# tanh(softplus(h)) by sigmoid, arctan and sine, four blocks at a time, in a fused attention and expert kernel

## The chip, the cores and the metric

The kernel runs on one core of a Trainium2 chip. A core has TensorE (PE: matrix products, results in PSUM), ScalarE (ACT: functions from a loaded table), VectorE (DVE), GpSimd (POOL) and SyncE (SP, which issues DMAs). Each engine takes its own instructions in the order in which they were written into its queue and waits where one of them is not ready. PSUM has 8 banks of 512 fp32 words per partition. The metric is the device time of the whole program in microseconds (us).

## The reference, cut to what matters

Three parts follow each other: an attention in which a query sees only the keys of its own cluster, a layer of 8 experts in which each token takes the one that its gate chooses, and a dense layer:

```
def _moe2_ref(x, w_in, w_out):
    h = x @ w_in                      # 1536 x 512 by 512 x 2048
    sp = np.where(h > 20.0, h, np.log1p(np.exp(np.minimum(h, 20.0))))
    g = h * np.tanh(sp)
    return g @ w_out                  # 1536 x 2048 by 2048 x 512
```

The change is in the line `g = h * np.tanh(sp)` alone. tanh(log(1 + e^h)) equals ((1 + e^h)^2 - 1) / ((1 + e^h)^2 + 1).

## The kernel before, in words

Every fp32 operand of a product is kept as two fp16 parts, a high and a low one, and a product is three matmuls (high by high, high by low, low by high), so that most results leave PSUM twice: ACT writes the high part, then DVE or POOL subtracts it and writes the low part.

The dense layer handles the 1536 tokens in six column groups q of 256 tokens (`QW`), three for each of the two batches. For one q, `h_units` makes 16 blocks of 128 x 256 (`f`, the rows of h); a block is 12 matmuls with the weights `win` (tile `h`, line 1005 in `mm3`). Two blocks fill one PSUM bank, and four such banks are in turn (`ps_2` has bufs=4). For every block a generator `mish` is put on the list `pend`, and `advance` moves all of them on by one step as the next blocks are written down. Its steps are: exp of h on ACT (L1097, tile `u`), a clamp on POOL (L1098), then on ACT the square (1 + e^h)^2 (L1103, tile `m`), Ln (L1105) and Exp of its negative (L1106, tile `L`: the reciprocal); on DVE h times a term (L1104, tile `hn`, the last reader of the PSUM bank), and one correction step of the reciprocal (L1109, L1110); on POOL the product (L1111); last the high part on ACT (L1115) and the low part on POOL (L115, in `psub`). The result goes to `gsl`, which lies in the tiles `xb` and `gx`. `o_units` multiplies it with `wout` (L1160, tile `o`, 24 matmuls for every four blocks) and writes the rows out (L1165, L1167).

The dense layer of the first column groups runs beside the expert layer of the second batch (`moe1`): its products are the tile `eps` (also L1005; two PSUM banks in turn), and their results leave through ACT (L963, L982) and DVE (L967, L989). The weights of an expert come by DMA in 512 KB pieces (`wf`) and are split by ACT (L916) and DVE (L920). In the same time `convs` turns `w_out` from 64-bit numbers into fp16 parts, in 16 pieces (L1025 to L1028 and L1033 on DVE, L1031 on ACT), and `gate(1)` sorts the tokens of the second batch (L700, L711, L718). The order in which all this is written down is set by `mix`, which takes the next unit from the part that is furthest behind its share. From there a scheduler orders the instructions of each engine, all but SP's, by its own timeline. So where a DVE instruction waits, or takes long, everything written behind it on DVE waits too.

All functions in the kernel before are in one table of ACT, loaded once (L560, at the start). `rest` repeats the computation for tokens over a capacity; its loops run no trip in the profiled execution.

Of the kernel before, what the change touches and what calls it, by code (L numbers as in the profile page):

```python
# [19 lines left out]
P = 128  # L20
# [4 lines left out]
def clustered_attention_moe_kernel(  # L25
# [110 lines left out]
    nc.gpsimd.memset(cst[:, 0:1], 1.0)  # L136
    nc.gpsimd.memset(cst[:, 1:2], -2.0794415416798357)
    mcol = cp.tile([P, OV], F32, name="mcol")
# [931 lines left out]
    def open_second():  # L1070
        m_p["m1"] = ctx.enter_context(tc.tile_pool(name="m1", bufs=1, side="right"))
        m_p["m2"] = ctx.enter_context(tc.tile_pool(name="m2", bufs=2, side="right"))
        m_p["ps"] = ctx.enter_context(tc.tile_pool(name="ps_2", bufs=4, space=PSUM, side="right"))
        m_p["wout"] = m_p["m1"].tile([P, 2, NF, DM], F16, name="wout")
        gx = m_p["m1"].tile([P, 8, 2, QW], F16, name="gx")
        nx = (T * ROW) // (2 * QW)
        for b in range(2):
            v_ = xb[b].rearrange("p t r -> p (t r)")[:, 0:nx * 2 * QW].rearrange("p (n a w) -> p n a w", a=2, w=QW)
            gsl[b] = [v_[:, n] for n in range(nx)] + [gx[:, 4 * b + n] for n in range(NF - nx)]

    pend = []
    g_done = set()
    C20 = 485165195.40979

# [6 lines left out]

    def mish(pt, gg, key, w_=QW):

        m2 = m_p["m2"]
        yield
        u = m2.tile([P, QW], F32, tag="u", name="u", bufs=3)[:, 0:w_]
        nc.scalar.activation(out=u, in_=pt, func=AF.Exp, scale=2.0 ** -17)  # L1097
        nc.gpsimd.tensor_scalar(out=u, in0=u, scalar1=C20, scalar2=0.0, op0=ALU.min, op1=ALU.max)  # L1098
        yield
        m = m2.tile([P, QW], F32, tag="n", name="m", bufs=4)[:, 0:w_]  # L1100
        L = m2.tile([P, QW], F32, tag="L", name="L", bufs=3)[:, 0:w_]
        hn = m2.tile([P, QW], F32, tag="hn", name="hn", bufs=4)[:, 0:w_]
# [10 lines left out]
        if key:  # L1113
            assert key[0] < 2 or (key[0] - 2, key[1] // 4) in o_done, key
        nc.scalar.activation(out=gg[:, 0], in_=hn, func=AF.Copy)  # L1115
        psub(gg[:, 1], hn, gg[:, 0])
        g_done.add(key)

# [4 lines left out]
    def h_units(q):  # L1123
# [4 lines left out]
        for f in range(NF):  # L1128
            while q > 1 and (q - 2, f // 4) not in o_done:
                yield None  # L1130
            if f % 2 == 0:
                h_t[q] = m_p["ps"].tile([P, 2, QW], F32, tag="h", name="h")
            pt = h_t[q][:, f % 2]
            mm3(pt, win, x1[:, :, :, p * QW:(p + 1) * QW], CD, slice(f * P, (f + 1) * P))
# [12 lines left out]
    def o_units(q):  # L1147
# [3 lines left out]
        for f4 in range(NF // 4):  # L1151
# [5 lines left out]
            for t in range(NQ):  # L1157
                for f in range(4 * f4, 4 * f4 + 4):
                    for i_, (a, c) in enumerate(((0, 0), (0, 1), (1, 0))):
                        nc.tensor.matmul(pts[t], lhsT=gsl[q % 2][f][:, a, t * P:(t + 1) * P], rhs=wout[:, c, f, :], start=(f == 0 and i_ == 0), stop=(f == NF - 1 and i_ == 2))  # L1160
                if t == NQ - 1:
                    o_done.add((q, f4))
                if f4 == NF // 4 - 1:
                    ob = m_p["m2"].tile([P, DM], F32, tag="ob", name="ob")
                    nc.scalar.activation(out=ob, in_=pts[t], func=AF.Copy, scale=-2.0 ** -17)  # L1165
                    tt = p * NQ + t
# [7 lines left out]
    def rest():  # L1174
# [194 lines left out]
```

## Time and profile before

| what | value |
|---|---|
| time, median of 3 runs | 718.24 us (718.12 to 718.4) |
| time of the profiled execution | 716.69 us |
| its span, first to last instruction | 715.0 us |
| mean granted TensorE clock | 0.962 |
| PE busy | 618.3 us (86%) |
| DVE busy | 545.8 us (76%) |
| ACT busy | 469.8 us (66%) |
| POOL busy | 448.7 us (63%) |

The shares are averages over parts of the program that have different limits: the attention takes about the first 340 us, the experts of the first batch lie partly in it, and the dense layer runs from 342.5 us to 706.3 us. PE's busy time counts every matmul that is on its way, so the cost of a matmul is read from the time between starts in a row of equal ones, not from the mean of one.

### The profile page before, as it was taken

The numbers are of one execution on the slowest core, as the hardware profiler recorded it, in microseconds if no ns is written. First come the engines' busy times: TensorE is split into PE (matmuls) and PEld (weight loads), VectorE is DVE, ScalarE is ACT, GpSimd is POOL, SyncE is SP. The second block draws the span as 40 slices with busy tenths as digits, with TensorE's granted clock in tenths as the row PEclk, the third lists the DMA queues.
The fourth block names the chain that finished last, engine by engine and source line by source line (L and its number), as shares of the span: only waits on it lengthen the run. The fifth ranks groups of instructions, "written<-read, shape, count | busy, mean of one in ns | idle before, by whom it ended". The sixth has DMA issues, their size and how long they took to land.

```text
span 715.0 us, 15063 instructions
## 1 busy us (share of the span) xinstructions
PE 618.3 (86%) x5618; PEld 409.0 (57%) x5619; DVE 545.8 (76%) x1047; ACT 469.8 (66%) x980; POOL 448.7 (63%) x516
## 2 busy tenths in 40 slices
PE   1697989976678895988998978799999999999995
PEld 1365767744356553654765555556666666776542
DVE  6889887899999999789969999996543356465400
ACT  2577888876467775664658786768755678777500
POOL 5578797995955656551276757656565577777711
PEclk9899999999689998999999999989999999999999
DMA  7542352413833332345344443351100000000000
GB/s 227 134 92 64 91 162 60 109 45 97 280 83 93 95 108 75 119 148 160 108 165 161 148 143 93 95 174 58 45 16 0 1 30 1 31 1 16 17 30 33
DMA packets 56753, 64.52 MB, mean 90 GB/s; under 512 B 10080, under 2 KB 46944, under 8 KB 56672
## 3 DMA queue, kind: packets, MB, share of 16 engines
q1 hardware_dynamic: 42064, 48.74, 24.1%
q10 hardware_dynamic: 12688, 8.42, 3.9%
q0 software_dynamic: 1920, 6.32, 2.3%
q8 instruction: 47, 0.77, 0.5%
q14 instruction: 34, 0.28, 0.1%
HBM read 46.23 MB, written 6.32 MB: 73 GB/s over the span
## 4 chain that ended last, share of the span: by engine, by line
PE 44%; DVE 34%; issue 9%; DMA 5%; ACT 4%; POOL 3%; SPq 1%; POOLq 0%; DVEq 0%; ACTq 0%
PE h L1005 13%; PE o L1160 11%; PE eps L1005 8%; DVE mxh L349 4%; DVE w L920 3%; DVE f L1026 3%; DMA wf<-in_moe_w_dram 2%; DVE f L1028 2%; PE s L389 2%; DVE mxh L354 2%; DVE f L1025 2%; DVE win L1033 2%; DVE oT L299 2%; PE x L348 1%; DVE m L363 1%
## 5 line engine op out<-in xcount | busy, mean ns | idle before, releaser
L115 POOL TENSOR_TENSOR el<-e,eh 128x768 f16<-128x768 f32 x86 | 146.7, 1716 | 62.5 <-ACT eh L398 36.2
L1005 PE MATMUL h<-x,win 128*128 128x256 f16 x1152 | 132.3, 273 | 0.0
L1005 PEld LDWEIGHTS <-win 128*128 128x128 f16 x1152 | 112.6, 98 | 19.1
L1005 PEld LDWEIGHTS <-w 128*128 128x128 f16 x768 | 75.5, 99 | 76.2 <-issue 22.8
L1111 POOL TENSOR_TENSOR hn<-hn,L 128x256 f32<-128x256 f32 x96 | 79.1, 826 | 34.9 <-DVE L L1110 33.3
L1160 PE MATMUL o<-wout,xb 128*128 128x512 f16 x432 | 96.7, 381 | 0.0
L391 ACT ACTIVATE e<-s 128x384 f32<-128x384 f32 x152 | 70.3, 486 | 27.4 <-PE s L389 23.4
L1005 PE MATMUL eps<-xw,w 128*128 128x416 f16 x384 | 76.9, 351 | 12.8 <-DVE x L989 6.2
L389 PE MATMUL s<-QK 128*128 128x384 f16 x320 | 81.5, 345 | 4.2 <-ACT e L391 4.0
L398 ACT ACTIVATE eh<-e 128x768 f16<-128x768 f32 x88 | 73.9, 845 | 16.9 <-PE av L427 7.9
L1109 DVE SCALAR_TENSOR_TENSOR m<-m,L 128x256 f32<-128x256 f32 x96 | 54.1, 565 | 38.0 <-ACT L L1106 37.1
L1098 POOL TENSOR_SCALAR u<-u 128x256 f32<-128x256 f32 x96 | 49.8, 519 | 52.5 <-ACT u L1097 46.5
L1005 PE MATMUL eps<-hT,w 128*128 128x416 f16 x384 | 72.5, 342 | 2.7 <-DVE hT L967 1.7
L115 POOL TENSOR_TENSOR xb<-hn,xb 128x256 f16<-128x256 f32 x72 | 57.4, 800 | 21.9 <-ACT xb L1115 20.1
L1160 PEld LDWEIGHTS <-xb 128*128 128x128 f16 x432 | 42.5, 98 | 48.8 <-issue 1.2
L425 PE MATMUL av<-vst,eh 128*128 128x65 f16 x528 | 64.0, 198 | 6.2 <-DVE xt L440 4.9
L349 DVE TENSOR_REDUCE mxh<-x 128x1 f32<-128x512 f32 x96 | 63.5, 674 | 4.9 <-PE x L348 4.7
L427 PE MATMUL av<-vst,el 128*128 128x65 f16 x528 | 61.3, 197 | 5.2 <-POOL el L115 4.6
L426 PE MATMUL av<-vst,eh 128*128 128x64 f16 x528 | 64.0, 199 | 0.0
L1104 DVE SCALAR_TENSOR_TENSOR hn<-m,h 128x256 f32<-128x256 f32 x96 | 39.3, 412 | 31.5 <-ACT m L1103 30.5
L1103 ACT ACTIVATE m<-u,cst 128x256 f32<-128x256 f32 x96 | 48.1, 502 | 20.2 <-POOL u L1098 19.0
L425 PEld LDWEIGHTS <-eh 128*128 128x128 f16 x528 | 51.1, 100 | 15.2 <-DVE xt L440 7.4
(227 smaller groups left out, 1316.4 us busy)
## 6 DMA issues: line engine op xcount, KB each, us to landing
wf<-in_moe_w_dram ACTq DMA_DIRECT2D x16, 512.0 KB, 4.5
raw<-in_moe_w_in_dram SPq DMA_DIRECT2D x16, 512.0 KB, 3.8
raw<-in_moe_w_out_dram SPq DMA_DIRECT2D x16, 512.0 KB, 3.6
wf<-in_moe_w_dram SPq DMA_DIRECT2D x16, 512.0 KB, 4.4
QK<-hl SPq DMA_DIRECT2D x32, 192.0 KB, 3.1
xs<-dr SPq DMA_DIRECT2D x12, 258.0 KB, 3.0
t<-in_k_dram SPq DMA_DIRECT2D x8, 384.0 KB, 4.1
t<-in_q_dram SPq DMA_DIRECT2D x8, 384.0 KB, 3.4
```

Of the source, the lines that this page charges most:

```text
L115: nc.gpsimd.tensor_tensor(out=out_, in0=in0, in1=in1, op=ALU.subtract)
L349: nc.vector.reduce_max(out=mx_t[i][:, t, 0:1], in_=sp, axis=AX.X)
L389: nc.tensor.matmul(sps[hf][:, 0:HS], lhsT=st[:, KA + a, kt * P:(kt + 1) * P], rhs=st[:, QA + a, hf * HS:(hf + 1) * HS], start=(a == 0), st ...
L391: nc.scalar.activation(out=e32[:, hf * HS:(hf + 1) * HS], in_=sps[hf][:, 0:HS], func=AF.Exp, scale=1.0 / float(D) ** 0.5)
L398: nc.scalar.activation(out=eh, in_=e32, func=AF.Copy)
L425: nc.tensor.matmul(av[:, t, :], lhsT=eh[:, cols], rhs=vs[:, h, 0:NV], start=(kt == 0 and t == 0), stop=False, skip_group_check=True)
L426: nc.tensor.matmul(av[:, t, 0:D], lhsT=eh[:, cols], rhs=vs[:, h, NV:], start=False, stop=False, skip_group_check=True)
L427: nc.tensor.matmul(av[:, t, :], lhsT=el[:, cols], rhs=vs[:, h, 0:NV], start=False, stop=(kt == T - 1), skip_group_check=True)
L1005: nc.tensor.matmul(out_, lhsT=wc[:, a, kk, ms], rhs=mv[:, c, kk, :], start=(i == 0), stop=(i == n - 1))
L1109: nc.vector.scalar_tensor_tensor(out=m, in0=m, scalar=1.0, in1=L, op0=ALU.add, op1=ALU.mult)
L1111: nc.gpsimd.tensor_tensor(out=hn, in0=hn, in1=L, op=ALU.mult)
L1160: nc.tensor.matmul(pts[t], lhsT=gsl[q % 2][f][:, a, t * P:(t + 1) * P], rhs=wout[:, c, f, :], start=(f == 0 and i_ == 0), stop=(f == NF - ...
```

## The change

tanh(log(1 + e^h)) is now computed as sin(2 arctan(sigmoid(h - log 2))). With s = e^h / (2 + e^h) the sine of twice the arctangent is 2s / (1 + s^2), which is the same fraction as before. ACT does sigmoid, arctan and sine, DVE one product with h, ACT and POOL the high and low part. The clamp and the correction step are gone. The work is grouped: one `mish` for four blocks, whose `h` tile takes two PSUM banks (two such tiles in turn, the same four banks in all). The sigmoid runs in two halves of 128 x 512, one for each bank; arctan, sine, the product and both parts are single instructions of 128 x 1024. Sigmoid and arctan are in one table of ACT and the sine in another, so that a group loads a table twice.

```
-    def mish(pt, gg, key, w_=QW):
+    def mish(pt, gg, q, k, n=FB, w_=QW):
         m2 = m_p["m2"]
-        yield
-        u = m2.tile([P, QW], F32, tag="u", name="u", bufs=3)[:, 0:w_]
-        nc.scalar.activation(out=u, in_=pt, func=AF.Exp, scale=2.0 ** -17)
-        nc.gpsimd.tensor_scalar(out=u, in0=u, scalar1=C20, scalar2=0.0, op0=ALU.min, op1=ALU.max)
-        yield
...
-        nc.scalar.activation(out=m, in_=u, func=AF.Square, bias=cst[:, 0:1])
-        nc.vector.scalar_tensor_tensor(out=hn, in0=m, scalar=-1.0, in1=pt, op0=ALU.add, op1=ALU.mult)
-        nc.scalar.activation(out=L, in_=m, func=AF.Ln, bias=cst[:, 0:1])
-        nc.scalar.activation(out=L, in_=L, func=AF.Exp, scale=-1.0, bias=cst[:, 1:2])
-        yield
-
-        nc.vector.scalar_tensor_tensor(out=m, in0=m, scalar=1.0, in1=L, op0=ALU.add, op1=ALU.mult)
-        nc.vector.scalar_tensor_tensor(out=L, in0=m, scalar=-0.25, in1=L, op0=ALU.add, op1=ALU.mult)
-        nc.gpsimd.tensor_tensor(out=hn, in0=hn, in1=L, op=ALU.mult)
-        yield
...
-        nc.scalar.activation(out=gg[:, 0], in_=hn, func=AF.Copy)
-        psub(gg[:, 1], hn, gg[:, 0])
+        s = m2.tile([P, FB, QW], F32, tag="s", name="s", bufs=3)[:, 0:n, 0:w_]
+        hf = max(n // 2, 1)
+        for u in range(0, n, hf):
+            nc.scalar.activation(out=s[:, u:u + hf], in_=pt[:, u:u + hf], func=AF.Sigmoid, scale=2.0 ** -17, bias=cst[:, 1:2])
+            if u + hf < n:
+                yield
+                yield
+        nc.scalar.activation(out=s, in_=s, func=AF.Arctan)
+        nc.scalar.activation(out=s, in_=s, func=AF.Sin, scale=2.0)
+        yield
+        nc.vector.scalar_tensor_tensor(out=s, in0=s, scalar=2.0 ** -6, in1=pt, op0=ALU.mult, op1=ALU.mult)
+        yield
...
+        nc.scalar.activation(out=gg[:, :, 0], in_=s, func=AF.Copy)
+        psub(gg[:, :, 1], s, gg[:, :, 0])
...
-            if f % 2 == 0:
-                h_t[q] = m_p["ps"].tile([P, 2, QW], F32, tag="h", name="h")
...
-            pend.append(mish(pt, gsl[q % 2][f], (q, f)))
-            next(pend[-1])
+            if f % FB == 0:
+                h_t[q] = m_p["ps"].tile([P, FB, QW], F32, tag="h", name="h", bufs=2)
...
+            if f % FB == 1:
+                pend.append(mish(h_t[q], gsl[q % 2][f // FB], q, f // FB))
+                next(pend[-1])
```

In the changed kernel the lines are L1101 (sigmoid), L1105 (arctan), L1106 (sine), L1108 (product on DVE) and L1111 (high part).

On ACT, at the first column group of the dense layer, this stands in the kernel before (`u`, `m` and `L` are the steps of the blocks of tile `h_5713` and of the next one, `wout` is a piece of `w_out`):

```order
L1097 ACTIVATE u_5738<-h_5713 128x256
L910 ISA
L910 DMA wf_6182<-in_moe_w2_dram 128x8x128
L1103 ACTIVATE m_5837<-u_5738,cst_112 128x256
L1105 ACTIVATE L_5838<-m_5837,cst_112 128x256
L1106 ACTIVATE L_5838<-L_5838,cst_112 128x256
L1097 ACTIVATE u_5844<-h_5713 128x256
L1097 ACTIVATE u_5869<-h_5824 128x256
```

and at the same place after the change (`s_5738` belongs to the first group of four, in `h_5713`, and `s_5935` to the second, in `h_5907`):

```order
L1101 ACT_TABLE_LOAD
L1101 ACTIVATE s_5738<-h_5713,cst_112 128x512
L910 ISA
L910 DMA wf_6082<-in_moe_w2_dram 128x8x128
L1101 ACTIVATE s_5935<-h_5907,cst_112 128x512
L1031 ACTIVATE wout_5627<-f32_6076 128x512
L1101 ACTIVATE s_5738<-h_5713,cst_112 128x512
L1105 ACTIVATE s_5738<-s_5738 128x1024
L1106 ACT_TABLE_LOAD
L1106 ACTIVATE s_5738<-s_5738 128x1024
L1101 ACT_TABLE_LOAD
L1101 ACTIVATE s_5935<-h_5907,cst_112 128x512
```

The first half of the second group's sigmoid now stands ahead of the second half of the first group's, so that the first group's banks are held until PE has done half of the second group. Two table loads stand in every group, 48 for the 24 groups.

On DVE, a little later, where the expert layer's last two `hT` pieces of the first batch are written, this stands in the kernel before:

```order
L967 SCALAR_TENSOR_TENSOR hT_5683<-eps_6090,hT_5683 128x416
L1176 CAST nf_10174<-nblk_139 128x16
L1109 SCALAR_TENSOR_TENSOR m_5974<-m_5974,L_5975 128x256
L1177 TENSOR_REDUCE nf_10174<-nf_10174 128x1
L1104 SCALAR_TENSOR_TENSOR hn_6047<-m_6045,h_5929 128x256
L1110 SCALAR_TENSOR_TENSOR L_5975<-m_5974,L_5975 128x256
L1178 TENSOR_SCALAR nblk_139<-nf_10174 128x1
L967 SCALAR_TENSOR_TENSOR hT_5683<-eps_6108,hT_5683 128x416
L920 SCALAR_TENSOR_TENSOR w_6381<-wf_6088,w_6381 128x1024
```

and after the change:

```order
L1108 SCALAR_TENSOR_TENSOR s_5738<-s_5738,h_5713 128x1024
L967 SCALAR_TENSOR_TENSOR hT_5683<-eps_6015,hT_5683 128x416
L1108 SCALAR_TENSOR_TENSOR s_5935<-s_5935,h_5907 128x1024
L967 SCALAR_TENSOR_TENSOR hT_5683<-eps_6033,hT_5683 128x416
L920 SCALAR_TENSOR_TENSOR w_6253<-wf_6013,w_6253 128x1024
```

Each of the two `hT` pieces now stands behind one group's product, which itself is behind that group's sine on ACT.

## Rows read from the trace of the kernel before

**Rows 1.** Busy time by stage; the columns are named in the first line.
```profile
core 0: us, PE busy (x) PEld busy (x) DVE busy (x) ACT busy (x) POOL busy (x), PEclk, DMA share, GB/s
342.50:394.10 51.60, 47.35 (x398) 34.91 (x397) 44.00 (x129) 35.57 (x85) 31.07 (x42) 1.00 0.42 138
394.10:463.90 69.80, 58.45 (x396) 38.53 (x395) 67.93 (x115) 51.59 (x116) 48.23 (x56) 0.99 0.39 121
463.90:545.00 81.10, 81.05 (x509) 50.52 (x509) 53.02 (x97) 56.57 (x133) 46.30 (x66) 0.97 0.21 66
545.00:664.70 119.70, 119.70 (x826) 80.64 (x824) 65.33 (x130) 87.08 (x220) 85.84 (x134) 1.00 0.04 14
664.70:706.30 41.60, 41.60 (x194) 18.69 (x192) 6.27 (x12) 9.59 (x23) 12.81 (x18) 1.00 0.04 15
```

**Rows 2.** PE's waits from 342.5 to 463.96 us: total us, times, longest.
```profile
PE eps L1005 <- DVE hT L967: 5.9, 4, 3.2
PE o L711 <- DVE dg L700: 4.2, 5, 1.5
PE eps L1005 <- DVE x L989: 3.7, 1, 3.7
PE eps L1005 <- ACT L L1105: 1.8, 2, 0.9
```

**Rows 3.** Timeline of PE around 460 us: start, length, instruction, idle before.
```profile
455.86 4.38 PE L1005 MATMUL eps<-hT,w 128*128 128x416 f16 x24
463.95 4.32 PE L1005 MATMUL eps<-xw,w 128*128 128x416 f16 x12 [3.71 <-DVE x L989]
```

**Rows 4.** Timeline of PE from 649 to 664.8 us.
```profile
649.06 5.40 PE L1005 MATMUL h<-x,win 128*128 128x256 f16 x48
654.30 5.34 PE L1160 MATMUL o<-wout,gx 128*128 128x512 f16 x24
```

**Rows 5.** ACT's groups, 342.5 to 463.9 us: count, busy us, mean ns, idle before.
```profile
L1103 ACT ACTIVATE m<-u,cst 128x256 f32<-128x256 f32 x30 | 15.0, 503 | 4.0 <-POOL u L1098 3.2 <-DVE goh L738 0.6
L1106 ACT ACTIVATE L<-L,cst 128x256 f32<-128x256 f32 x29 | 14.5, 502 | 0.2
L1105 ACT ACTIVATE L<-m,cst 128x256 f32<-128x256 f32 x29 | 14.4, 501 | 0.3
L916 ACT ACTIVATE w<-wf 128x1024 f16<-128x1024 f32 x12 | 12.7, 1055 | 1.8 <-DMA wf<-in_moe_w_dram 1.8
L1097 ACT ACTIVATE u<-h 128x256 f32<-128x256 f32 x30 | 10.4, 379 | 7.0 <-DVE hn L1104 6.9
L1115 ACT ACTIVATE xb<-hn 128x256 f16<-128x256 f32 x24 | 9.8, 410 | 8.2 <-POOL hn L1111 8.0
```

**Rows 6.** DVE's groups in the same stretch.
```profile
L1109 DVE SCALAR_TENSOR_TENSOR m<-m,L 128x256 f32<-128x256 f32 x29 | 17.7, 616 | 1.5 <-ACT L L1106 1.5
L920 DVE SCALAR_TENSOR_TENSOR w<-wf,w 128x1024 f16<-128x1024 f32 x12 | 17.5, 1460 | 0.3 <-ACT w L916 0.3
L1110 DVE SCALAR_TENSOR_TENSOR L<-m,L 128x256 f32<-128x256 f32 x29 | 13.7, 476 | 0.2
L1104 DVE SCALAR_TENSOR_TENSOR hn<-m,h 128x256 f32<-128x256 f32 x29 | 11.7, 407 | 0.3 <-ACT m L1103 0.3
```

**Rows 7.** POOL's groups: two of the same stretch, one of the attention.
```profile
L1111 POOL TENSOR_TENSOR hn<-hn,L 128x256 f32<-128x256 f32 x29 | 27.2, 942 | 15.0 <-DVE L L1110 14.2 <-DVE gm L766 0.4
L115 POOL TENSOR_TENSOR xb<-hn,xb 128x256 f16<-128x256 f32 x24 | 22.2, 934 | 10.2 <-ACT xb L1115 9.9
...
L115 POOL TENSOR_TENSOR el<-e,eh 128x768 f16<-128x768 f32 x86 | 146.7, 1716 | 62.5 <-ACT eh L398 36.2 <-PE s L389 10.1 <-issue 6.7
```

**Rows 8.** The one table load: duration ns (least, median, most), start.
```profile
L560 ACT ACT_TABLE_LOAD  x1: 1283/1283/1283, 0.8 to 0.8; - x1
```

**Rows 9.** ACT's copy of 128x512 from PSUM, 545 to 664.7 us.
```profile
L1165 ACT ACTIVATE ob<-o 128x512 f32<-128x512 f32 x6 | 3.5, 592 | 2.6 <-PE o L1160 2.6
```

**Rows 10.** Timeline of ACT: two instructions that follow each other without a wait.
```profile
646.00 0.49 ACT L1103 ACTIVATE m<-u,cst 128x256 f32<-128x256 f32 x1
646.40 0.49 ACT L1106 ACTIVATE L<-L,cst 128x256 f32<-128x256 f32 x1
```

More of the change, by code (lines that the diff above doesn't have):

```diff
@@ L136, in clustered_attention_moe_kernel @@
     nc.gpsimd.memset(cst[:, 0:1], 1.0)
-    nc.gpsimd.memset(cst[:, 1:2], -2.0794415416798357)
+    nc.gpsimd.memset(cst[:, 1:2], -0.6931471805599453)
     mcol = cp.tile([P, OV], F32, name="mcol")
@@ L1078, in open_second @@
             v_ = xb[b].rearrange("p t r -> p (t r)")[:, 0:nx * 2 * QW].rearrange("p (n a w) -> p n a w", a=2, w=QW)
-            gsl[b] = [v_[:, n] for n in range(nx)] + [gx[:, 4 * b + n] for n in range(NF - nx)]
+            assert nx % FB == 0 and NF - nx <= FB
+            gsl[b] = [v_[:, n:n + FB] for n in range(0, nx, FB)] + [gx[:, FB * b:FB * (b + 1)]]
     pend = []
     g_done = set()
-    C20 = 485165195.40979
+    FB = 4
     def advance():
@@ L1159, in o_units @@
                     for i_, (a, c) in enumerate(((0, 0), (0, 1), (1, 0))):
-                        nc.tensor.matmul(pts[t], lhsT=gsl[q % 2][f][:, a, t * P:(t + 1) * P], rhs=wout[:, c, f, :], start=(f == 0 and i_ == 0), stop=(f == NF - 1 and i_ == 2))
+                        nc.tensor.matmul(pts[t], lhsT=gsl[q % 2][f // FB][:, f % FB, a, t * P:(t + 1) * P], rhs=wout[:, c, f, :], start=(f == 0 and i_ == 0), stop=(f == NF - 1 and i_ == 2))
                 if t == NQ - 1:
@@ L1164, in o_units @@
                     ob = m_p["m2"].tile([P, DM], F32, tag="ob", name="ob")
-                    nc.scalar.activation(out=ob, in_=pts[t], func=AF.Copy, scale=-2.0 ** -17)
+                    nc.scalar.activation(out=ob, in_=pts[t], func=AF.Copy, scale=2.0 ** -17)
                     tt = p * NQ + t
@@ L1223, in rest @@
                 for f in range(NF):
-                    pt = ps2.tile([P, P], F32, tag="h", name="h")
-                    mm3(pt, win, x1, CD, slice(f * P, (f + 1) * P))
-                    for _ in mish(pt, gsl[0][f][:, :, 0:P], None, P):
+                    pt = ps2.tile([P, 1, P], F32, tag="h", name="h", bufs=2)
+                    mm3(pt[:, 0], win, x1, CD, slice(f * P, (f + 1) * P))
+                    for _ in mish(pt, gsl[0][f // FB][:, f % FB:f % FB + 1, :, 0:P], None, f, 1, P):
                         pass
@@ L1230, in rest @@
                     for i_, (a, c) in enumerate(((0, 0), (0, 1), (1, 0))):
-                        nc.tensor.matmul(po, lhsT=gsl[0][f][:, a, 0:P], rhs=wout[:, c, f, :], start=(f == 0 and i_ == 0), stop=(f == NF - 1 and i_ == 2))
+                        nc.tensor.matmul(po, lhsT=gsl[0][f // FB][:, f % FB, a, 0:P], rhs=wout[:, c, f, :], start=(f == 0 and i_ == 0), stop=(f == NF - 1 and i_ == 2))
                 ob = m2.tile([P, DM], F32, tag="ob", name="ob")
-                nc.scalar.activation(out=ob, in_=po, func=AF.Copy, scale=-2.0 ** -17)
+                nc.scalar.activation(out=ob, in_=po, func=AF.Copy, scale=2.0 ** -17)
                 nc.gpsimd.indirect_dma_start(out=out, out_offset=bass.IndirectOffsetOnAxis(ap=iu[:, 1:2], axis=0), in_=ob, in_offset=None, bounds_check=NT - 1, oob_is_err=False)
```

12 lines of the change are left out of this document (4 added, 8 removed).

## The prediction

> **What bounds the kernel now.** I read the busy times by stage first, because the shares over the whole span say nothing here: nothing before 342.5 us belongs to the changed code, and there the order of PE is the same in both kernels. From 463.9 us to 706.3 us PE is busy without a gap (81.05 of 81.1, 119.7 of 119.7, 41.6 of 41.6 us) [rows 1]. What another engine saves there is worth nothing, and only a new wait of PE would show. In the two stages from 342.5 to 463.9 us PE is busy 47.35 + 58.45 = 105.8 of 121.4 us, and in the second of them DVE is busy 67.93 of 69.8 us [rows 1]. So 15.6 us is what PE loses in all.
>
> Second, who releases PE there: hT on DVE 5.9 us, dg on DVE 4.2, x on DVE 3.7, ACT's Ln 1.8, together 15.6 us [rows 2]. All but the last name DVE. PE waits for a short DVE instruction that stands in a full queue. Third, the timeline after the longest of these waits: 12 matmuls of the form eps took 4.32 us there, where 24 had taken 4.38 us just before [rows 3]. That is the lower of the clock's two levels (1.2 against 2.4 GHz) after PE had stood still for 3.71 us; the granted clock of that stage is 0.97 where the neighbours have 0.99 and 1.00 [rows 1]. It costs 4.32 - 2.19 = 2.1 us. So at most 15.6 + 2.1 = 17.7 us can be had. A kernel without any wait of PE behind 342.5 us would end at about 716.7 - 17.7 = 699 us.
>
> **The change, part by part.** DVE: a block now costs L1109, L1110 and L1104, 616 + 476 + 407 ns, in that stretch 17.7 + 13.7 + 11.7 = 43.1 us [rows 6]. The two column groups that lie there make eight groups of four, and each gets one product of 128x1024. Its nearest row is L920, the same operation at that width, 1.46 us [rows 6]; four of the L1104, which read PSUM as it does, make 1.63 us. With 1.5 us the eight cost 12 us. DVE loses 43 - 12 = 31 us of the 112 us that it is busy in the two stages [rows 1] and is no longer the bound.
>
> POOL: a block now has the product (942 ns), the low part (934 ns) and the clamp. What is left is one low part for four blocks, between 1.72 us (the 128x768 form) and 4 x 0.93 = 3.7 us [rows 7]. POOL waits less, and nobody waits for it: only what o needs much later comes from there.
>
> ACT: a block now costs 379 + 503 + 501 + 502 + 410 ns, so four blocks 9.18 us [rows 5]. A group after the change has two sigmoids of 128x512, arctan, sine and the copy at 128x1024, and two table loads. No row shows the three functions. For the sigmoid the nearest row is the copy of 128x512 from PSUM, 0.59 us [rows 9], plus what an operand for the bias adds (L1103 with one takes 503 ns and L1097 without one 379 ns [rows 5], 0.12 us): 0.71 us. At 128x1024 the nearest row is L916, 1.055 us [rows 5]. So the group takes 1.42 + 3.17 us. The load has one row, 1.283 us [rows 8], and I take that, 2.57 us for two. The sum is 7.15 us, 2.0 us below before. Instructions that follow each other without a wait start 0.40 us apart where each lasts 0.49 [rows 10], so both sums are a little high. The Trainium skill, "ScalarE: Activation LUTs", section "Step-by-step: what each stage is for", says that each function takes the same time per element; no run here shows it yet.
>
> The lower end for the functions is the plain copy, and an upper end would be four times the 128x256 rows, 4 x 0.50 = 2.0 us at 128x1024. A group would then cost 2 x 1.0 + 2 x 2.0 + 1.64 + 2.57 = 10.2 us, 1.0 us more than before. I take the wide row, since L916 shows directly what that width costs.
>
> From 545 us on, PE needs 10.4 us for a group (48 matmuls of h start 5.24 us before 24 of o, which take 5.2 [rows 4]). ACT's 7.15 us, and 0.3 us for the copies of o, lie beneath that. In that part a group's banks are wanted again only after 24 o, 48 h and 24 o, 15.6 us after its last matmul. The way from that matmul to the end of the product is 0.71 + 1.06 + 1.28 + 1.06 + 1.5 = 5.6 us. It fits, and so nothing is won or lost behind 463.9 us.
>
> In the stage from 342.5 to 463.9 us ACT has 35.57 + 51.59 = 87.2 us of work [rows 1], of which 15.0 + 14.5 + 14.4 + 10.4 + 9.8 = 64 us (and 1.7 us of the same copies into gx) is this function's [rows 5]. After: 8 x 7.15 = 57 us, so about 79 us beside 106 us of matmuls.
>
> What is late next, then? I followed the order after the change with these durations through the first groups. The first group's second sigmoid stands behind the first one of the second group. That one waits 4.4 us from the first group's last matmul (7 eps, the 12 small ones of the ranks and 24 h lie between), and then come 0.71, a wout piece (0.6, as [rows 9]), 0.71, 1.06, 1.28, 1.06 and the product's 1.5: 11.3 us. PE asks for the banks after 48 h, 24 eps and the ranks, 5.2 + 4.4 + 0.5 = 10.1 us. That is a wait of 1 us, or 3 where DVE is not free. The last hT piece of the first batch stands on DVE behind the product of the second group, and PE's last three matmuls that use it come about 1 us early. In the part where the second batch's first expert runs, ACT's half of hT stands up to 0.71 + 1.06 + 1.28 + 1.06 = 4.1 us behind a group's sigmoid, arctan, load and sine, but between two eps of the same bank stand 12 other eps (2.2 us) and 12 to 27 h (1.3 to 3 us), so that a wait of under 1 us is left, a few times. The waits for the sorted rows' DMA behind dg stay (about 1 us), and so may one for expert weights. I put 7 us of waits in place of the 17.7 us and get a gain of 10.5 us.
>
> The profiled execution took 716.69 us (span 715.0 and 1.7 around it), which is 1.55 us under the median of 718.24. So 716.7 - 10.5 = 706.2 us on the profile's scale, and **707.7 us** as the median of runs. The likeliest case's own range is 703 to 713, from 15 down to 5 us of gain.
>
> **The rivals.**
> First, that a table load costs more than its row. The one load stood at the program's start with nothing before it on ACT; in the new places it stands between instructions that overlap now (0.49 us long, 0.40 apart [rows 10]), and what the engine does not start while the load waits for the one before it is in no row. If each load holds ACT for twice its row, the 16 loads of the stage add 16 x 1.28 = 20.5 us: 99 us of work on an engine that also waits for PE and DVE. It idles 121.4 - 87.2 = 34 us there now; if half of that remains, the stage lasts 99 + 17 + 2.6 (until the first half group is there) = 118.6 us, 2.8 us less than now, and the time is 715.4 us, between 712 and 719. Behind 545 us the group would take 9.7 us of 10.4 and still fit. For it: the loads are in order and cannot overlap. Against it: the row itself is a complete load.
> The Trainium skill, "ScalarE: Activation LUTs", section "What ACT_TABLE_LOAD costs", gives 1283 ns for the load, as the trace has it, and another 1380 ns for a drain ahead of it, 2.66 us for each switch; by that an estimate for 16 loads is 22 us more on ACT, and the time would be this rival's. No run here shows the drain.
>
> Second, slower: the banks are held too long. With two tiles of two banks PE can be one group ahead; before, it could be three tiles ahead and each was free after one exp, a clamp, a square and one DVE product. A group's way to the end of its product is 5.6 us at best, and 48 h matmuls fill only 5.2 us of it. Whatever stands before it on ACT (the last group's copy 1.06, a split of weights 1.06, a load 1.28, an hT 0.5: 3.9 us) is waited for by PE unless eps or dg lie between. It decides from 17.7 / 8 = 2.2 us of wait per group on. With 2.7 us in each of eight groups, and the low clock's 2.1 us after one of them, it costs 21.6 + 2.1 = 23.7 us against 17.7: 6 us slower, 724 us, from 720 to 727. For it: the first group, as followed above. Against it: in these stages 24 eps or 24 dg matmuls stand between the two halves of most groups, which is 2 to 4 us of cover each.
>
> Third, no change: DVE's waits come back as ACT's. hT, x and xw all pass through ACT before DVE, and ACT's instructions in front of them become twice to four times as long. If PE's 15.6 us stay as they are under ACT's name, the time is 718 us, 716.8 to 719.5. For it: PE's one wait for ACT now is for an Ln of this function (1.8 us [rows 2]). Against it: ACT has less to do than DVE had, 79 us against 112.
>
> **How the numbers follow.** Forecast 0.60, expensive loads 0.17, held banks 0.15, no change 0.08. Faster or slower begins at 0.2% (1.4 us), which is what a measurement of this kernel can tell from none. The forecast is faster in all its range; of the expensive loads 0.11 lies under 716.8 us, 0.04 within and 0.02 above; of no change 0.06 within and 0.01 on each side; held banks is slower. Faster 0.71 (0.60 + 0.11, rounded down for the last), same 0.10, slower 0.19. The low end, 701, leaves 1.7 us of waits over the floor on the runs' scale (699 + 1.55); the high end, 720, takes in the expensive loads and no change, and leaves out most of held banks.
>
> **What would show it.** Right: DVE's busy time falls by about a quarter of 112 us between 342 and 460 us; PE's waits for hT and x on DVE shrink to about 1 us each; the dense stage that is now free of gaps starts about 10 us earlier and still has none; the sigmoid lasts about 0.7 us, arctan and sine about 1.05, a load 1.28 with under 0.3 us of other idle time beside it. Wrong: a gap of 1 us or more on ACT around each load (first rival); waits of h on the product L1108 of more than 2 us, again and again (second); waits of eps on ACT's L963 or L982 that add up to 15 us (third); or any gap of PE behind the expert layer.

## The result, and the profile after

The changed kernel takes **708.07 us** (median of 4 runs, 704.72 to 709.14) against 718.18 us for the kernel before beside it (4 runs, 717.21 to 718.4). The ratio is 0.9843, with a 95% interval from 0.981 to 0.9877: 10.1 us faster, where 10.5 us had been forecast. A control later gave 707.39 us.

The profiled execution took 704.72 us. Its attention ended 2 us earlier than before's, which is no part of the change (its order of PE is the same). So I compare the *dense stage*: from the start of the first product of h to the end of the last product of o. It took 363.7 us before (342.5 to 706.2) and 354.2 us after (340.5 to 694.7), 9.5 us less; the control had 354.2 us again.

Busy times by stage after, which answer to [rows 1] and have its columns:

```profile
340.50:390.50 50.00, 47.19 (x399) 34.78 (x397) 37.08 (x107) 38.06 (x52) 14.62 (x12) 1.00 0.46 152
390.50:454.80 64.30, 58.06 (x395) 38.31 (x394) 54.01 (x70) 47.56 (x62) 10.30 (x5) 1.00 0.48 156
454.80:545.00 90.20, 90.20 (x581) 56.73 (x580) 22.15 (x27) 52.90 (x63) 16.89 (x11) 1.00 0.12 36
545.00:652.00 107.00, 107.00 (x740) 72.12 (x738) 11.56 (x11) 70.37 (x75) 25.46 (x16) 1.00 0.04 16
652.00:694.40 42.40, 42.40 (x210) 20.43 (x209) 2.44 (x2) 10.27 (x12) 7.20 (x5) 1.00 0.04 13
```

In the first two stages PE is busy 105.25 us (105.8 before), but of 114.3 us instead of 121.4: it idles 9.05 us where it idled 15.6. DVE falls from 111.9 to 91.1 us, ACT from 87.2 to 85.6, POOL from 79.3 to 24.9. From 454.8 us on PE has no gap. The granted clock is 1.00 in all five; the low clock after the long wait [rows 3] is gone. Over the dense stage PE's idle time fell by 6.6 us (15.65 to 9.05) and its busy time by 2.9 us (348.05 to 345.15).

PE's waits from 342 us to the end, against [rows 2] (total us, times, longest):

```profile
PE eps L1005 <- DVE hT L967: 3.6, 4, 2.1
PE h L1005 <- ACT s L1101: 2.8, 4, 1.2
PE h L1005 <- DVE s L1108: 1.5, 2, 0.8
PE o L711 <- DVE dg L700: 1.1, 1, 1.1
```

The wait for x (3.7 us) is gone, hT and dg are smaller, and h now waits, 4.3 us in all: 1.5 us for the last reader of its banks (L1108), and 2.8 us for a sigmoid (L1101). ACT's groups of the function over the dense stage, against [rows 5] and [rows 8]:

```profile
L1101 ACT ACTIVATE s<-h,cst 128x512 f32<-128x512 f32 x48 | 33.0, 687 | 62.6 <-PE h L1005 62.4
L1101 ACT ACT_TABLE_LOAD x24 | 30.8, 1283 | 2.4 <-PE h L1005 2.0
L1106 ACT ACT_TABLE_LOAD x24 | 30.8, 1283 | 0.4
L1106 ACT ACTIVATE s<-s 128x1024 f32<-128x1024 f32 x24 | 25.4, 1057 | 0.3
L1105 ACT ACTIVATE s<-s 128x1024 f32<-128x1024 f32 x24 | 25.3, 1056 | 0.7
```

DVE's and POOL's groups from 340.5 to 454.8 us, against [rows 6] and [rows 7]:

```profile
L1026 DVE SCALAR_TENSOR_TENSOR f<-raw,f 128x512 int32<-128x512 int32 x16 | 17.9, 1122 | 0.3
L920 DVE SCALAR_TENSOR_TENSOR w<-wf,w 128x1024 f16<-128x1024 f32 x13 | 16.5, 1272 | 0.2 <-ACT w L916 0.2
...
L1108 DVE SCALAR_TENSOR_TENSOR s<-s,h 128x1024 f32<-128x1024 f32 x7 | 8.6, 1222 | 12.2 <-ACT s L1106 12.2
...
L115 POOL TENSOR_TENSOR xb<-s,xb 128x1024 f16<-128x1024 f32 x6 | 13.5, 2247 | 43.6 <-ACT xb L1111 43.5
```

L1026 splits the weights of wout and has nothing to do with the change. Its mean is 1122 ns, and the reason is in the next timelines (start, length, instruction, idle before): first POOL's only instruction from 410 to 425 us, then DVE, ACT and PE beside it.

```profile
418.00 2.12 POOL L115 TENSOR_TENSOR xb<-s,xb 128x1024 f16<-128x1024 f32 x1 [19.09 <-ACT xb L1111]
```
```profile
418.16 2.51 DVE L1026 SCALAR_TENSOR_TENSOR f<-raw,f 128x512 int32<-128x512 int32 x1
420.70 0.69 DVE L1028 SCALAR_TENSOR_TENSOR f<-raw,f 128x512 int32<-128x512 int32 x1
422.09 0.69 DVE L1033 SCALAR_TENSOR_TENSOR wout<-f,wout 128x512 f16<-128x512 f32 x1 [0.69 <-ACT wout L1031]
422.70 0.58 DVE L967 SCALAR_TENSOR_TENSOR hT<-eps,hT 128x416 f16<-128x416 f32 x1
```
```profile
421.43 0.63 ACT L1031 ACTIVATE wout<-f 128x512 f16<-128x512 f32 x1 [3.51 <-DVE f L1028]
421.97 0.50 ACT L963 ACTIVATE hT<-eps 128x416 f16<-128x416 f32 x1
```
```profile
423.34 2.27 PE L1005 MATMUL eps<-xw,w 128*128 128x416 f16 x12 [2.13 <-DVE hT L967]
```

L1026 starts 0.16 us after POOL's subtraction and ends 0.55 us after it (420.12 to 420.67): it lasts 2.51 us instead of 0.69, as if it stood still until POOL had ended. L1028 follows it, ACT's wout piece waits 3.51 us for that, ACT's hT stands behind the wout piece, and PE loses 2.13 us, its longest wait.

### The profile page after: what moved, and what is told of

It is laid out like the page before. It is cut to its first block, busy times and chain, and to the rows that moved or that the text cites. A ratio compares the mean times of both kernels' runs of the same rounds, so it can differ in the third digit from the quotient of the medians.

```text
span 703.1 us, 14009 instructions
## 1 busy us (share of the span) xinstructions
PE 616.4 (88%) x5618; PEld 408.3 (58%) x5619; DVE 433.1 (62%) x783; ACT 448.4 (64%) x668; POOL 299.1 (43%) x252
## 4 chain that ended last, share of the span: by engine, by line
PE 42%; DVE 32%; issue 9%; ACT 6%; DMA 5%; POOL 2%; SPq 1%; POOLq 0%; DVEq 0%; ACTq 0%
PE h L1005 12%; PE o L1157 12%; PE eps L1005 7%; DVE mxh L349 4%; DVE f L1026 4%; DVE w L920 3%; DVE f L1028 2%; DMA QK<-oT 2%; PE s L389 2%; DVE oT L299 2%; DVE mxh L354 2%; DVE f L1025 2%; DVE win L1033 2%; PE x L348 1%; DMA wf<-in_moe_w_dram 1%
## 5 line engine op out<-in xcount | busy, mean ns | idle before, releaser
L1108 DVE SCALAR_TENSOR_TENSOR s<-s,h 128x1024 f32<-128x1024 f32 x24 | 29.3, 1221 | 167.7 <-ACT s L1106 165.1
L115 POOL TENSOR_TENSOR xb<-s,xb 128x1024 f16<-128x1024 f32 x18 | 39.6, 2201 | 142.9 <-ACT xb L1111 142.7
L1005 PE MATMUL eps<-xw,w 128*128 128x416 f16 x384 | 75.1, 344 | 6.2 <-DVE hT L967 3.2
L1101 ACT ACTIVATE s<-h,cst 128x512 f32<-128x512 f32 x48 | 33.0, 687 | 62.6 <-PE h L1005 62.4
L425 PEld LDWEIGHTS <-eh 128*128 128x128 f16 x528 | 51.1, 100 | 15.8 <-DVE xt L440 8.0
L427 PEld LDWEIGHTS <-el 128*128 128x128 f16 x528 | 51.1, 102 | 11.9 <-POOL el L115 7.1
L426 PEld LDWEIGHTS <-eh 128*128 128x128 f16 x528 | 51.1, 100 | 3.8 <-issue 0.8
L348 PE MATMUL x<-QK 128*128 128x512 f16 x96 | 40.6, 431 | 12.7 <-DVE mxh L349 6.9
```

The source lines that it names most:

```text
L115: nc.gpsimd.tensor_tensor(out=out_, in0=in0, in1=in1, op=ALU.subtract)
L348: nc.tensor.matmul(sp, lhsT=st[:, QA, t * P:(t + 1) * P], rhs=st[:, KA, 0:512], start=True, stop=True)
L425: nc.tensor.matmul(av[:, t, :], lhsT=eh[:, cols], rhs=vs[:, h, 0:NV], start=(kt == 0 and t == 0), stop=False, skip_group_check=True)
L426: nc.tensor.matmul(av[:, t, 0:D], lhsT=eh[:, cols], rhs=vs[:, h, NV:], start=False, stop=False, skip_group_check=True)
L427: nc.tensor.matmul(av[:, t, :], lhsT=el[:, cols], rhs=vs[:, h, 0:NV], start=False, stop=(kt == T - 1), skip_group_check=True)
L1005: nc.tensor.matmul(out_, lhsT=wc[:, a, kk, ms], rhs=mv[:, c, kk, :], start=(i == 0), stop=(i == n - 1))
```

## The experiments

| kernel | us (median) | ratio to before (95%) | dense stage | PE idle in it |
|---|---|---|---|---|
| before | 717.7 to 718.2 | 1 | 363.7 | 15.65 |
| changed | 708.07 | 0.9843 (0.981 to 0.9877) | 354.2 | 9.05 |
| control x0 | 707.39 | 0.985 (0.9814 to 0.9886) | 354.2 | 8.95 |
| x1 one table | 701.23 | 0.9762 (0.9743 to 0.9782) | 348.1 | 3.65 |
| x2 twice the loads | 716.97 | 0.9995 (0.9964 to 1.0027) | 364.2 | 14.4 |
| x3 before, less DVE | 706.54 | 0.9834 (0.9797 to 0.9871) | 353.1 | 8.1 |
| x4 before, less POOL | 703.82 | 0.981 (0.9792 to 0.9827) | 351.4 | 6.6 |
| x5 DVE's work back | 711.27 | 0.9911 (0.9895 to 0.9928) | 358.9 | 10.6 |
| x9 POOL's work back | 714.77 | 0.996 (0.993 to 0.9991) | 361.9 | 14.1 |
| x6 low part on DVE | 703.69 | 0.9776 (0.9722 to 0.9831) | 350.0 | 5.5 |
| x6b the same again | 702.92 | 0.9783 (0.9746 to 0.9821) | 349.5 | 4.9 |
| x8 fours, one table | 706.41 | 0.9841 (0.9799 to 0.9883) | 353.7 | 8.8 |
| x10 x8, low part on DVE | 700.76 | 0.9754 (0.9718 to 0.979) | 347.2 | 3.1 |
| x7 groups of two | 732.04 | 1.0199 (1.0155 to 1.0244) | 377.3 | 25.1 |

The last two columns are one row by windows for each kernel, from its first h to its last o (length, and length less PE's busy time). Each is from one profile; two profiles of the changed kernel agree there within 0.1 us, and the two of x6 within 0.6. The stage grows by idle time and also by PE's own busy time, which runs from 344.1 us (x10) to 352.2 (x7): after long waits the granted clock was lower (x2 and x7 below).

**What the table loads cost.** x1 has arctan in the sine's place, x2 a one-column sine ahead of the arctan (no load and four loads for a group instead of two):

```
-        nc.scalar.activation(out=s, in_=s, func=AF.Sin, scale=2.0)
+        nc.scalar.activation(out=s, in_=s, func=AF.Arctan, scale=2.0)
```


> The changed kernel with the sine replaced by a second arctan, so that two table loads are left in place of 48 in the dense layer; PE's order is the same, and the output is not the reference's. If the gain comes from DVE's shorter queue and the loads lie beneath PE's matmuls, as the prediction has it: at most 3 us under the changed kernel's 708.1, 705 to 708. If the loads are what still holds PE up (the first rival, loads dearer than their row): 702 us or less, and PE's waits for L1101, L1108 and L967 go from 8 us to 2 or less.


```
+        dm = m2.tile([P, 1], F32, tag="dm", name="dm", bufs=3)
+        nc.scalar.activation(out=dm, in_=s[:, 0, 0:1], func=AF.Sin)
```


> The changed kernel with a sine of one column between sigmoid and arctan, so that a group loads four tables in place of two (the column's result is not used). Without the two loads the time was 701.2 us, with them 708.1. If a load costs through ACT's queue in the stage that has gaps of PE: again 5 to 8 us, 713 to 717 us, and behind the expert layer PE still has no gap, since ACT's 10.1 us for a group are just beneath PE's 10.4. If the loads only took ACT's idle time there: 708 to 710 us.

Measured: the dense stage is 348.1, 354.2 and 364.2 us with 0, 2 and 4 loads for a group. The first pair of loads costs 6.1 us, the second 10.0. x1's gain is more than the prediction's account allowed (at most 3 us) and fits the other expectation, 702 us or less; x2 is at the upper end of its first. PE idles 3.65 us in x1, and h no longer waits for ACT or for its banks (first the stage, then PE's waits):

```profile
343.80:691.90 348.10, 344.45 (x2318) 222.48 (x2315) 130.57 (x216) 158.26 (x214) 73.22 (x49) 1.00 0.20 66
```
```profile
PE eps L1005 <- DVE hT L967: 2.3, 2, 1.3
PE o L711 <- DVE dg L700: 1.0, 2, 0.7
```

In idle time the two pairs cost the same: 5.4 us (3.65 to 9.05) and 5.35 (9.05 to 14.4). The second pair also adds 4.6 us to PE's busy time (345.15 to 349.79), at the lower clock: in x2 the granted clock is 0.94 from 342 to 395 us and 0.97 from there to 460, and 24 matmuls of h take 4.45 us after a wait of 2.39 us, where 24 take 2.78 elsewhere. x2's first stage:

```profile
342.00:395.00 53.00, 47.74 (x383) 35.07 (x381) 35.71 (x106) 47.64 (x62) 14.59 (x12) 0.94 0.43 146
```

But a load does not hold ACT for more than its row. ACT's timeline of the changed kernel, one group:

```profile
350.85 1.06 ACT L1105 ACTIVATE s<-s 128x1024 f32<-128x1024 f32 x1
351.93 1.28 ACT L1106 ACT_TABLE_LOAD   x1
353.22 1.06 ACT L1106 ACTIVATE s<-s 128x1024 f32<-128x1024 f32 x1
354.30 1.28 ACT L1101 ACT_TABLE_LOAD   x1
355.59 0.69 ACT L1101 ACTIVATE s<-h,cst 128x512 f32<-128x512 f32 x1
```

Each load starts 0.02 us after the instruction before it ends, and the next starts 0.01 us after the load; besides the 1.283 us only the usual overlap of two instructions (0.1 us) is lost. The 1380 ns of drain that the Trainium skill gives ("ScalarE: Activation LUTs", section "What ACT_TABLE_LOAD costs") is not in this trace; its 1283 ns is. So the price comes from ACT's order, in which the next group's sigmoid, hT and the wout pieces stand behind the loads; that is read from the order and from the waits that x1 removes. One link can be seen in the timelines, ACT first:

```profile
363.31 1.28 ACT L1101 ACT_TABLE_LOAD   x1
364.60 0.69 ACT L1101 ACTIVATE s<-h,cst 128x512 f32<-128x512 f32 x1
```
```profile
365.34 0.93 PE L1005 MATMUL h<-x,win 128*128 128x256 f16 x7 [1.20 <-ACT s L1101]
```

All four waits of h for L1101 (2.8 us) end like this, 0.05 us after a sigmoid that stands directly behind a load. This one is not for the banks of a group before: the last product L1108 ahead of it ended at 362.20 us. In the code the sigmoid of a group's first half is written ahead of the matmuls of its second half, and both are in one tile, so that PE waits for the sigmoid of its own group. That the common tile is the reason is read from the code and not tested; x7, where a group is whole before its sigmoid, has no wait of h.

**Was it DVE's work or POOL's that had bound the kernel before?** Two kernels made from the one before, each with one of the two taken out (so each leaves a part of the function out):

```
-        nc.vector.scalar_tensor_tensor(out=m, in0=m, scalar=1.0, in1=L, op0=ALU.add, op1=ALU.mult)
-        nc.vector.scalar_tensor_tensor(out=L, in0=m, scalar=-0.25, in1=L, op0=ALU.add, op1=ALU.mult)
```


> The kernel before without the correction step, L1109 and L1110 on DVE (the reciprocal of L1106 is used as it is; that part of the computation is left out). ACT, POOL and the banks stay as they were. If DVE's own instructions were the bound: DVE loses 31.4 us of the stretch from 342 to 464 us, and most of the gain is there, 706 to 711 us. If it was POOL that stretched DVE's instructions and held up the rest: POOL is as busy as before, and the time stays at 714 to 718 us.


```
-        nc.gpsimd.tensor_scalar(out=u, in0=u, scalar1=C20, scalar2=0.0, op0=ALU.min, op1=ALU.max)
...
-        nc.gpsimd.tensor_tensor(out=hn, in0=hn, in1=L, op=ALU.mult)
...
-        nc.scalar.activation(out=gg[:, 0], in_=hn, func=AF.Copy)
-        psub(gg[:, 1], hn, gg[:, 0])
+        nc.scalar.activation(out=gg[:, 0], in_=L, func=AF.Copy)
+        psub(gg[:, 1], L, gg[:, 0])
```


> The kernel before without POOL's clamp and product (L1098 and L1111; the high and low part are taken from the result of L1110, so that all of DVE's and ACT's instructions stay and the values are not the reference's). POOL loses 46 of 79 us of its work in the stretch. If DVE's own instructions were the bound: little, 714 to 718 us. If POOL stretched them (L1109 took 616 ns there and 420 elsewhere) or its part of the chain held the banks: 706 to 711 us, with L1109, L1026 and L920 shorter by a fifth or more.

Measured: 10.6 us off the dense stage without DVE's two operations, 12.3 us without POOL's two. Either one is worth the whole change. x4 keeps every DVE instruction of before, and they became shorter: the two corrections (L1108 and L1109 in x4) 439 and 444 ns instead of 616 and 476 [rows 6].

```profile
L1108 DVE SCALAR_TENSOR_TENSOR m<-m,L 128x256 f32<-128x256 f32 x32 | 13.9, 439 | 0.2
```

Only the first of them became shorter by a fifth, as expected: L920 fell by 12% (1460 to 1286 ns) and L1026 by 5% (809 to 766). x3's time lies in the range for DVE's own instructions, x4's 2 us under the one for POOL, and neither excludes the other. x4 is not a clean test of POOL beside DVE alone, since it also takes away ACT's waits for POOL (3.2 and 8.0 us in [rows 5]); the next ones are nearer to that.

**Is either alone enough to take the gain back?** Eight dummy operations of 128x256 for each group, on DVE (x5) or on POOL (x9, products instead):

```
...
+                nc.vector.scalar_tensor_tensor(out=xd[:, 0], in0=s[:, u], scalar=1.0, in1=s[:, u], op0=ALU.add, op1=ALU.mult)
+                nc.vector.scalar_tensor_tensor(out=xd[:, 1], in0=xd[:, 0], scalar=-0.25, in1=s[:, u], op0=ALU.add, op1=ALU.mult)
```


> The changed kernel with eight additional DVE instructions of 128x256 in each group, which only read the result and write a tile that nobody uses: DVE gets back what the correction step took, about 3.4 us for each group or 27 us in the stretch. If the gain is DVE's shorter queue: it is gone, 714 to 719 us. If it came from POOL's smaller work or from the grouping on ACT: 707 to 710 us.

> The changed kernel with eight additional POOL products of 128x256 in each group, which only read the result and write a tile that nobody uses: POOL gets back about what the change took from it (8 x 0.8 = 6 us for each group), DVE and ACT are left alone. If POOL's work holds DVE up (in the profile after, one DVE instruction of L1026 lasts 2.5 us beside POOL's low part and 0.69 without it): 711 to 716 us, with L1026, L920 and L1028 longer by a fifth or more. If only DVE's own work counts: 707 to 710 us.

Measured: the dense stage is 4.7 us longer with DVE's work back (the time lies between the two expectations), 7.7 us with POOL's. In idle time of PE that is 1.55 and 5.05 us; the rest is PE's busy time at a lower clock (granted 0.97 in x5 up to 460 us, 0.98 in x9 from 395 to 463.9). In x5 DVE is busy 234.9 us of the stage, as long as in the kernel before (236.6), and the stage is still 4.8 us shorter than before; in x9 DVE is busy 143.3 us, and it is only 1.8 us shorter. Neither PE nor ACT nor DVE waits for POOL by a semaphore anywhere in x9's dense stage, yet L920 takes 1712 ns in its first part instead of 1272, and L1028 888 instead of 687:

```profile
L920 DVE SCALAR_TENSOR_TENSOR w<-wf,w 128x1024 f16<-128x1024 f32 x12 | 20.6, 1712 | 0.0
L1026 DVE SCALAR_TENSOR_TENSOR f<-raw,f 128x512 int32<-128x512 int32 x16 | 13.5, 845 | 0.3
```

L1026 did not become longer, as was expected, but shorter (845 ns instead of 1122): its longest is 1.10 us there instead of 2.61, while its median rose from 692 to 802 ns.

**The low part on DVE.** Nothing is left out here; the only POOL instruction of the function moves to DVE, which is busier for it:

```
-        psub(gg[:, :, 1], s, gg[:, :, 0])
+        nc.vector.tensor_tensor(out=gg[:, :, 1], in0=s, in1=gg[:, :, 0], op=ALU.subtract)
```


> The changed kernel with the low part of each group made by DVE (about 1.2 us) in place of POOL (2.2 us). If POOL beside DVE costs more than it takes off it: the 2.5 us instructions of L1026 are gone and the time falls to 704 to 707 us. If DVE's work by count decides: eight more instructions of 1.2 us, 709 to 711 us.

> The changed kernel again, unaltered, as the control of this set: 708 us, 704 to 711; its dense stage (from the start of the first product of h in the profile to the end of the last product of o) 354 us, as in the profile before. Both theories expect the same; what it shows is how far one kernel moves from one set of runs to the next, which the other three need.

> The changed kernel with the low part subtracted on VectorE instead of GpSimd, a second time, beside its own control. Theory GpSimd (its operations beside VectorE's lengthen these): 4 us under the control (the dense stage 350 against 354), 702 to 705, a ratio of .977 to .981. Rival (the first time it was the chip that differed): level with the control within 1.5 us.

Measured twice: 4.2 and 4.7 us off the dense stage, 4.5 us off the median beside its own control (702.92 to 707.39; the intervals of the ratios overlap by 0.0007). The first time's 703.69 us is just under its range. PE's waits in x6b differ from the changed kernel's mainly in one line, that for hT, which falls from 3.6 us to 0.2:

```profile
PE h L1005 <- ACT s L1101: 2.5, 4, 1.1
PE h L1005 <- DVE s L1108: 1.3, 1, 1.3
PE o L711 <- DVE dg L700: 0.9, 1, 0.9
PE eps L1005 <- DVE hT L967: 0.2, 1, 0.2
```

The same line of both kernels (duration in ns: least, median, most), changed kernel first, x6b second:

```profile
L1026 DVE SCALAR_TENSOR_TENSOR f<-raw,f x16: 682/692/2608, 341.1 to 450.8; 128x512 int32<-128x512 int32 x16
```
```profile
L1026 DVE SCALAR_TENSOR_TENSOR f<-raw,f x16: 678/688/694, 345.7 to 452.5; 128x512 int32<-128x512 int32 x16
```

DVE has 18 us more to do in the dense stage (145.29 against 127.24 us), and L1026's long instructions are gone.

**Is it the new function or the grouping?** x8 keeps the old functions (exp, square, Ln, exp: one table) in groups of four with clamp and products on DVE, without the correction step, and with one buffer for each of its tiles in place of three; x10 has the low part on DVE as well, so that POOL computes nothing of it:

```
...
+        nc.vector.tensor_scalar(out=u_, in0=u_, scalar1=485165195.40979, scalar2=0.0, op0=ALU.min, op1=ALU.max)
+        nc.scalar.activation(out=u_, in_=u_, func=AF.Square, bias=cst[:, 0:1])
+        nc.vector.scalar_tensor_tensor(out=s, in0=u_, scalar=-1.0, in1=pt, op0=ALU.add, op1=ALU.mult)
...
+        nc.vector.tensor_tensor(out=s, in0=s, in1=L, op=ALU.mult)
```


> The groups of four and the two banks as in the changed kernel, but with the functions of the kernel before, which are all in one table: exp (two halves), square, Ln, Exp on ACT, clamp and two products on DVE, only the low part on POOL, no correction step. No table is loaded in the dense layer; ACT has 5.3 us for each group in place of 7.15, DVE about 3.2 in place of 1.2. If the gain is fewer and wider instructions on DVE and POOL, and the sine brings nothing but two loads for each group: 701 to 705 us. If the shorter DVE queue of the sine is what counts: 708 to 712 us.

> Groups of four with exponential and logarithm from one table (no loads in the stage) and with both the clamp and the low part on VectorE: GpSimd computes nothing of the activation. VectorE then has a clamp, two products and a subtraction for four blocks. Theory (loads cost 6 us, GpSimd's subtraction 4, a VectorE operation of this kind 1 to 2 a group): the kernel of groups of four with one table lay level with the changed one and gains 4 from the subtraction: 702, 700 to 705, the dense stage 350. Rival (VectorE is the bound there again, since clamp and first product stand ahead of it): no gain from the move, 706 to 709, with the products of o and eps waiting for VectorE.

Measured: x8 is level with the changed kernel, 353.7 us against 354.2 in the dense stage, and its time (706.41 us) lies between the two expectations; the sine and arctan, with their loads, bring nothing that the old functions in groups of four without the correction don't. What the grouping itself brings is not shown: x3, with blocks one by one, no loads and no correction, has a dense stage of 353.1 us, as short as x8's. x10 takes 6.5 us off x8's dense stage, more than the 4 expected: 700.76 us, faster than both kernels. Of the versions that leave out nothing at all, x6 (measured again as x6b) is the shortest. x10's waits of PE:

```profile
PE o L711 <- DVE dg L700: 2.4, 2, 1.5
PE eps L1005 <- DVE hT L967: 0.3, 1, 0.3
PE h L1005 <- DVE s L1109: 0.2, 1, 0.2
```

What is left in x10 is 3.1 us of idle time; the dense stage's matmuls alone take 344.1 us.

**Groups of two**, one bank each, with twice the loads (four h tiles in turn instead of two, four tiles `s` instead of three, and one step instead of two between the halves of a sigmoid):

```
-    FB = 4
+    FB = 2
...
```


> The changed kernel with groups of two blocks in one bank each instead of four in two: 48 groups, so twice the loads, and ScalarE's and VectorE's operations half as long. Theory loads (two more of 1.28 us for four blocks cost what two more cost as an added sine, 9 us): 717, 714 to 722, the dense stage 363, products of h waiting for ScalarE. Rival (what the grouping costs is the holding of two banks, and banks freed sooner give it back): 708 to 713, the waits of h for VectorE's product gone.

Measured: 732.04 us, beyond both expectations. Its longest waits of PE:

```profile
PE eps L1005 <- DVE hT L967: 15.6, 7, 8.1
PE o L1155 <- ACT ob L1160: 4.5, 2, 4.3
```

No wait of h is left, neither for its banks nor for ACT, so that half of the rival's claim holds, but it saves little. What grew is the wait for hT, which passes through ACT. The expectation priced the two more loads as x2 did; the sigmoids were cut in two halves as well (96 of 471 ns, busy 40.3 us in all, instead of 48 of 687, 33.0). ACT's sum over the dense stage rises to 300.1 us from 219.2 (285.2 in x2), and its queue is late behind the expert layer too, where the changed kernel has no gap. Beside 16 us more of idle time PE's busy time is 7.1 us longer (352.2 us): after the wait of 8.1 us 24 matmuls of eps take 7.09 us, where 24 take 4.38 elsewhere:

```profile
368.27 7.09 PE L1005 MATMUL eps<-hT,w 128*128 128x416 f16 x24 [8.13 <-DVE hT L967]
```

How the 23 us divide among the loads, the cut sigmoids and the rest is not shown.

## Why the prediction was right, and where it was not

*The ceiling.* 17.7 us of idle time and low clock were said to be all that can be had. x10's dense stage is 16.5 us shorter and still idles 3.1: 19.6 us in all. Right within 2 us; no kernel went further.

*The clock.* The 2.1 us of half clock fell away; PE's busy time fell by 2.9 us (by 3.9 in x10). Right, if a little small.

*DVE as the bound, and its relief.* DVE's busy time fell by 20.8 us of 112, a fifth and not a quarter, and ACT's came to 85.6 us where 79 had been put. Both sums took durations out of a busy time in which the overlap of neighbours counts once. The durations of all groups, added up, fell by 28.5 us on DVE (130.5 to 101.9) and by 9.5 on ACT (101.6 to 92.1), near the 31 and 8 of the forecast. x3 shows that DVE's relief alone brings 10.6 us. Right in kind, but the reason was half of it: a part of what the rows charged to DVE was POOL's. In the kernel before, the instruction with an operand in PSUM, L1104, never lasts longer than 422 ns, and L1109 of the same shape with both in SBUF lasts up to 945:

```profile
L1104 DVE SCALAR_TENSOR_TENSOR hn<-m,h x31: 402/406/422, 348.3 to 467.9; 128x256 f32<-128x256 f32 x31
...
L1109 DVE SCALAR_TENSOR_TENSOR m<-m,L x30: 409/611/945, 349.6 to 466.4; 128x256 f32<-128x256 f32 x30
```

If their shortest durations are taken as their own, (616 - 410) x 29 + (1460 - 1220) x 12 ns = 8.9 us of the stage [rows 6] are an estimate of what these two lines lost beside POOL; without two of POOL's three instructions (x4) 7.2 us of it were gone ((616 - 439) x 29 + (1460 - 1286) x 12 ns).

*POOL.* "POOL waits less, and nobody waits for it" is the step that failed. By semaphores it is true that nobody waits for it; but DVE's instructions lengthen beside POOL's. x4, x9, x6 and x10 show it from both sides: 12.3 us gained, 7.7 lost, 4.2 to 4.7 and 6.5 gained. The Trainium skill states a rule for it ("SBUF — State Buffer", section "SBUF: two separate sides"): a DVE operation with two inputs in SBUF and a GpSimd operation that reads SBUF share a port pair, and the later one waits until the other has ended. The trace agrees (0.69 us became 2.51, ending 0.55 us after POOL). The step should have asked what POOL's instructions do to DVE's. The change gained from this, since POOL's work fell by 54 us in the two stages, and lost from it, since the one long subtraction that remains comes between the wout pieces. That is why the waits for hT did not shrink to about 1 us, as the signs had it: 3.6 us were left, and without the subtraction on POOL 0.2 (x6b).

*DVE's product.* 1.5 us was put from L920; it takes 1.222 us. L920's mean of 1460 ns held the lengthening (its median after is 1218), so the row was the right one and the value in it was not.

*ACT's group.* 0.71, 1.055 and 1.283 us were put; 0.687, 1.057 and 1.283 came. The group is 2 x 0.687 + 3 x 1.056 + 2 x 1.283 = 7.1 us. Right. A gap of 1 us or more beside each load, the sign of the first rival, is not there.

*The waits in place of the old ones.* 7 us were put, 9.05 came: the banks 1.5 us (1 to 3 put), hT 3.6, dg 1.1, and 2.8 us for which there was no term, of a group's second half for the sigmoid of its first half behind a load. The term for ACT was too small ("a wait of under 1 us is left, a few times"): x1 shows that without the loads only 3.65 us are left, so 5.4 of the 9.05 us of idle time go back to them. The first rival was right that the loads are dear and wrong in how: ACT is held for the row and no more.

*Behind the expert layer* no gap came, as said. *Held banks*: 1.5 us behind the product L1108 in 2 waits, none over 0.8; the second rival did not happen.

So the sum came out because its terms were near: of old idle time and low clock 17.7 us were put and 18.6 went (15.65 and 2.9), of new waits 7 were put and 9.05 came. The first term came out partly by luck. DVE's own shorter work was to make the old waits go, and POOL's smaller work had no place in the sum. With dummy work on POOL in its place (x9) 1.8 of the 9.5 us are left, and with dummy work on DVE (x5) 4.8: without POOL's relief, which the change brought along, little of the forecast gain would have come. How much each of the two weighs inside the 10.1 us is not settled: x3, x4 and x6 are not additive (no kernel's stage was under 347 us, 344 of them matmuls), and dummy work need not lie where the old work lay.

## What to carry to other kernels

When an engine seems to be the bound, look at the least, median and longest duration of one of its lines, all of one shape. If the longest is far from the least (945 against 409 ns, 2608 against 682 here), see in the timelines what another engine ran in that moment: taking work from *that* engine can pay without a semaphore between the two. Moving an instruction from GpSimd to DVE can pay even though DVE gets busier. A table load costs what its row says on ACT, but its price to the kernel is what stands behind it in ACT's order, and the low clock after the longer waits; here the old functions from one table, in groups of four and without the correction step, brought as much as the new functions.

## What the runs showed of the hardware that was not expected

The lengthening goes both ways between the two engines. First DVE, then POOL:

```profile
395.48 1.45 DVE L920 SCALAR_TENSOR_TENSOR w<-wf,w 128x1024 f16<-128x1024 f32 x1
396.85 2.61 DVE L1026 SCALAR_TENSOR_TENSOR f<-raw,f 128x512 int32<-128x512 int32 x1
```
```profile
395.84 3.07 POOL L115 TENSOR_TENSOR gx<-s,gx 128x1024 f16<-128x1024 f32 x1
```

DVE's L920 starts beside a short POOL instruction and takes 1.45 us instead of 1.22. POOL's subtraction starts while L920 runs and lasts 3.07 us instead of 2.1. DVE's L1026, behind L920, ends at 399.46, 0.55 us after POOL. The times fit three instructions in a row that each paid for the one before. The DVE lines that read PSUM (L1104, L1108, L967) kept their durations within 5% in the first two stages of both kernels. Two tensor inputs do not seem to be needed for it: L700, which reads one tensor and a small operand, takes 1.13 us instead of 0.24 where it starts at 364.73 us beside a subtraction of POOL's that runs from 363.37 to 365.82.

```profile
L700 DVE TENSOR_SCALAR dg<-ident,xs x12: 239/242/1132, 364.7 to 381.3; 128x128 f16<-128x128 f16 x12
```
